# Own places for the parts of xu, one place for two scratch tiles, and another table of biases in a planned kernel

## The chip, the cores and the metric

The kernel runs on one core of a Trainium2 chip. The time is device microseconds (us) of one execution. TensorE is PE in the rows, VectorE is DVE, ScalarE is ACT, GpSimd is POOL, and SyncE, which issues the DMAs, is SP. A row's PEclk is the granted clock of TensorE as a share of full speed.

## The reference

Three computations follow one another, all in fp32, for 4 batches of 768 positions and 384 channels (8 heads of 48).

```python
# 1. attention with a complex decay; a is scaled so that |a| <= 0.999
for t in range(S):
    new_re = ar * S_re - ai * S_im
    new_im = ar * S_im + ai * S_re
    S_re, S_im = new_re + kv, new_im          # kv = outer(k_t, v_t)
    y[:, :, t] = einsum('bhd,bhde->bhe', q[:, :, t], S_re)
# 2. mixing over the positions (rank 32), then a channel MLP 384 -> 1536 -> 384
u = x + (x^T @ U @ V)^T
x = u + relu(u @ w_ch1) @ w_ch2
# 3. a gate from a causal convolution of 5 taps
gate = sigmoid(sum_k conv_w[k] * x shifted by 4 - k)
out = (gate * (x @ w_val)) @ w_out
```

## The kernel before, in words

**The work.** The attention goes through 12 units, three for each batch b, of 256 positions each, named by their first position: (b, 0), (b, 256), (b, 512). A unit (`attention`, line 763) reads the decay into z, normalises it (xa), forms running products over groups of 8 positions (the prefix steps, lines 809 to 814: two products s1 and s2, then z), carries the products over the groups (the phase steps, lines 820 to 892: un, tot, cx, fs, t), scales q and k with them (xc), transposes them on PE (pst, into qT and kT), and runs chunks of 128 positions as matmuls: pss (q times k), masked by DVE to mt; pkv, the state st; py, the output yt. yt goes to memory, and by pxt, xo and pxu into xu, the product of x and U.

The rest (`moe`, line 1042) goes by batch and by half hf of 384 positions; (0,1) is half 1 of batch 0. At the start of a batch, xu is split into a large part xh and a small part xl = xu - xh, and both are copied into xuh (lines 1043 to 1053). For each half: three matmuls pu of xuh; DVE adds them to the input xt; ACT makes the large part of m3u and DVE the small one (`pair`, line 1036). Matmuls of full precision are three passes: large by large, large by small, small by large. Twelve blocks then go through ph (9 matmuls), hp (large part on ACT, small on DVE) and px (9 matmuls). Behind the last px, DVE adds px to xt; ACT makes the large parts of m3x, DVE the small ones; ACT does the first tap and DVE the four others of each of the three convolutions (g, 12 steps in all), ACT the sigmoid; pv (27 matmuls), g times pv, m3g; po (27 matmuls), and the result ob is written.

**The weights** come as 64-bit numbers. DVE and ACT turn them into fp32 (`single`, line 678: wt by one TENSOR_SCALAR and two SCALAR_TENSOR_TENSOR for each of 28 tiles) and split them into two parts (w) while the first attention units run.

**Places.** `T` (line 521) asks for a tile in a named place with a number of buffers. A tile that takes a used buffer waits until all operations on the holder before have ended (lines 145 to 155). Before, xh takes a place of m3 (three buffers, shared with m3u, m3x and m3g), xl and jkx one of ob (two buffers, shared with the results). The phase steps' scratch has a place of its own, t1; the prefix steps use s1 and s2.

**The order.** No operation is issued when the program's text names it. `add` (line 176) records it; `order` (line 244) lays all operations out as a list schedule, and `emit` issues each engine's operations in that order. An operation's urgency is its longest remaining path, plus a bias from the table `URGE` (line 117), by kind and engine: "m00V" is DVE's work of half (0,0), "a10P" PE's work of the first unit of batch 1, "sV", "w0A" small inputs and weights.

```python
bias = [self.URGE.get(op.kind + op.eng, 0.0) for op in self.ops]
...
start, end = self.lay([x + y for x, y in zip(urgency, bias)])
...
return sorted(self.ops, key=lambda o: (o.start, o.i))
```

So a place that changes its name takes some waits away and adds others, and another table changes the order on all engines. On an engine, instructions run in the order in which they were issued.

Of the kernel before, what the change touches and what calls it, by code (L numbers as in the profile page):

```python
# [10 lines left out]
F32 = mybir.dt.float32  # L11
F32R = mybir.dt.float32r
# [88 lines left out]
class Program:  # L101
# [32 lines left out]
    }  # L134

    def hop(self, d, u):
# [363 lines left out]
def chunked_path(ctx, tc, outer, q, k, v, a_re, a_im, moe_U, moe_V, w1, w2, w_val, conv_w, w_out, out):  # L500
# [260 lines left out]
    XN = DM * RK // 128  # L761
# [461 lines left out]
```

## Time and profile before

| | |
|---|---|
| time, median of 3 | 757.41 us (753.73 to 758.91) |
| profiled execution | 754.51 us, span 752.6 us |
| PE busy | 627.3 us (83%), 4354 matmuls |
| DVE busy | 622.9 us (83%), 1545 instructions |
| ACT busy | 449.0 us (60%), 1110 instructions |
| mean granted clock of PE | 0.94 |
| chain that ended last | PE 53%, DVE 30%, DMA 6%, ACT 5% |

The profile shows one execution. Its rows of a timeline give start, duration, engine, line, operation, output and inputs, count, and in brackets the idle time of the engine before the row and what ended it. A row of windows gives the length, the busy time of each engine, the mean granted clock, the share of DMA and its rate. The first moe half, (0,0), gets its first m3u at 163.4 us, and the later halves at 239.8, 334.4, 405.2, 491.1, 550.9 and 643.1 us; PE's last px ends at 723.1 us. Stages are cut at these marks.

### The profile page before, as it was taken

Reading aid. Unit: us, or ns where it says so; the run is one execution under the profiler, and the core shown is the slowest. Engines: PE = TensorE matmul, PEld = TensorE weight load, DVE = VectorE, ACT = ScalarE, POOL = GpSimd, SP = SyncE. Lnnn points to the kernel's source line nnn. Section 1 sums busy time; section 2 is a strip of 40 time slices with the busy share of each in tenths; the row PEclk is TensorE's granted clock in tenths of the full one; section 3 lists DMA queues with packets and bytes.
Section 4 is the critical chain, followed back from the end, with each engine's and each line's share of the span. In section 5 each row is a group of like instructions: output and inputs, shape, how many; then the busy total and the mean of one; then the engine's idle time right before and its main releaser. Section 6 shows DMA issues by size and latency. Waiting matters only on the chain.

```text
span 752.6 us, 12213 instructions
## 1 busy us (share of the span) xinstructions
PE 627.3 (83%) x4354; PEld 577.5 (77%) x4354; DVE 622.9 (83%) x1545; ACT 449.0 (60%) x1110; POOL 2.7 (0%) x31
## 2 busy tenths in 40 slices
PE   0002959969978999889989999899899999999994
PEld 0002848749967989869988999789799998899984
DVE  5999999999999989799799899995799885515261
ACT  6899877673585564774665565851865355414243
POOL 1000000000000000000000000000000000000000
PEclk9999559869997999889999999999999999999997
DMA  5992315520521361430411544303124331100001
GB/s 120 305 369 65 76 21 138 126 54 0 139 51 53 85 151 35 126 101 22 127 43 54 148 112 130 84 23 105 43 74 120 82 84 33 54 0 1 1 32 36
DMA packets 74676, 64.39 MB, mean 86 GB/s; under 512 B 46704, under 2 KB 62064, under 8 KB 74608
## 3 DMA queue, kind: packets, MB, share of 16 engines
q1 hardware_dynamic: 74608, 63.54, 31.4%
q8 instruction: 36, 0.59, 0.3%
q14 instruction: 32, 0.26, 0.1%
HBM read 47.00 MB, written 16.52 MB: 84 GB/s over the span
## 4 chain that ended last, share of the span: by engine, by line
PE 53%; DVE 30%; DMA 6%; ACT 5%; SPq 3%; issue 2%; DVEq 0%; ACTq 0%
PE ph L600 18%; PE px L600 16%; DVE g L567 4%; PE po L600 3%; DVE z L551 3%; DVE xc L551 3%; PE pst L621 3%; PE py L612 3%; SPq L631 3%; PE pss L600 3%; DVE s L551 3%; DVE wt L567 2%; DVE xa L551 2%; PE pv L600 2%; PE pkv L612 2%
## 5 line engine op out<-in xcount | busy, mean ns | idle before, releaser
L600 PE MATMUL ph<-m3u,w 128*128 128x384 f32 x864 | 210.6, 353 | 4.2 <-ACT m3u L589 2.5
L600 PE MATMUL px<-hp,w 128*128 128x384 f32 x864 | 201.1, 343 | 0.6 <-DVE xt L551 0.4
L600 PEld LDWEIGHTS ph<-m3u,w 128*128 128x128 f32 x864 | 157.1, 194 | 10.9 <-ACT m3u L589 4.4
L600 PEld LDWEIGHTS px<-hp,w 128*128 128x128 f32 x864 | 153.1, 188 | 3.5 <-issue 1.7
L589 ACT ACTIVATE hp<-ph 128x384 fp32r<-128x384 f32 x96 | 46.7, 489 | 110.2 <-PE ph L600 100.4
L567 DVE SCALAR_TENSOR_TENSOR hp<-ph,hp 128x384 fp32r<-128x384 f32 x96 | 52.8, 552 | 58.8 <-ACT hp L589 58.3
L600 PE MATMUL pss<-qT,kT 96*128 96x128 f32 x384 | 54.7, 290 | 1.9 <-ACT qT L589 1.9
L551 DVE TENSOR_TENSOR s<-xa,z 128x192 f32<-128x192 f32 x168 | 54.3, 348 | 0.8 <-ACT z L589 0.3
L600 PEld LDWEIGHTS pss<-qT,kT 96*128 96x128 f32 x384 | 51.1, 202 | 4.0 <-ACT qT L589 2.6
L567 DVE SCALAR_TENSOR_TENSOR g<-xt,cw,g 128x384 f32<-128x384 f32 x96 | 52.9, 609 | 0.4 <-ACT g L589 0.3
L600 PE MATMUL pv<-m3x,w 128*128 128x384 f32 x216 | 45.6, 352 | 6.3 <-DVE m3x L551 5.1
L621 PE MATMUL pst<-eye_r,xc 128*96 128x128 f32 x192 | 32.1, 295 | 20.1 <-DVE rt L551 17.8
L589 ACT ACTIVATE xa<-xa,cb 128x384 f32<-128x384 f32 x72 | 42.9, 610 | 4.9 <-DVE xa L567 3.2
L600 PEld LDWEIGHTS pv<-m3x,w 128*128 128x128 f32 x216 | 37.1, 190 | 9.6 <-DVE m3x L551 7.0
L621 PEld LDWEIGHTS pst<-eye_r,xc 128*96 128x96 f32 x192 | 24.0, 137 | 23.0 <-ACT xa L589 18.0
L589 ACT ACTIVATE kT<-pst 96x512 f32<-96x512 f32 x48 | 27.3, 593 | 21.2 <-PE pst L621 21.0
L612 PE MATMUL py<-mt,vt 128*64 128x128 f32 x384 | 39.5, 296 | 0.1
L612 PEld LDWEIGHTS pkv<-vt,ks 128*96 128x96 f32 x320 | 34.0, 186 | 5.8 <-DVE mt L551 3.6
L612 PE MATMUL pkv<-vt,ks 128*96 128x48 f32 x320 | 34.5, 267 | 4.0 <-DVE mt L551 3.1
L551 DVE TENSOR_TENSOR mt<-pss,cmask 128x512 f32<-128x512 f32 x48 | 32.5, 683 | 5.6 <-PE pss L600 5.2
L612 PE MATMUL py<-qT,st 96*64 96x128 f32 x320 | 35.3, 301 | 0.6 <-ACT xo L589 0.6
L621 PE MATMUL psT<-eye_r,qd 128*96 128x128 f32 x24 | 5.3, 297 | 36.0 <-ACT qd L589 36.0
(161 smaller groups left out, 1178.8 us busy)
## 6 DMA issues: line engine op xcount, KB each, us to landing
raw<-in_moe_w_ch_dram SPq DMA_DIRECT2D x24, 384.0 KB, 7.2
kd<-z SPq DMA_DIRECT2D x18, 384.0 KB, 3.9
ks<-kd SPq DMA_DIRECT2D x15, 384.0 KB, 4.2
z<-in_a_re_dram SPq DMA_DIRECT2D x12, 384.0 KB, 4.5
z<-in_a_im_dram SPq DMA_DIRECT2D x12, 384.0 KB, 5.3
qk<-in_k_dram SPq DMA_DIRECT2D x12, 384.0 KB, 4.2
qk<-in_q_dram SPq DMA_DIRECT2D x12, 384.0 KB, 5.1
vt<-in_v_dram SPq DMA_DIRECT2D x24, 192.0 KB, 2.9
```

Source lines behind the costliest of these rows:

```text
L551: e, cost, lambda: engines[e].tensor_tensor(out=real(o), in0=real(a), in1=real(b), op=op), views(a, b), [o]
L567: lambda: nc.vector.scalar_tensor_tensor(out=real(o), in0=real(a), scalar=real(s), in1=real(b), op0=o0, op1=o1),
L589: return nc.scalar.activation(real(o), real(a), func, scale=real(scale), **kw)
L600: "P", cost, lambda: nc.tensor.matmul(real(o), real(lhsT), real(rhs), start=start, stop=stop),
L612: r = nc.tensor.matmul(ro[idx], real(lhsT), real(rhs), start=start, stop=stop)
L621: op = g.add("P", cost, lambda: nc.tensor.transpose(real(o), real(a), real(idn)), views(a, idn), [o])
L631: "S", cost, lambda: nc.sync.dma_start(real(o), real(a)), views(a), views(o), lat=1700.0 + time - cost
```

## The change

Three things are edited. In `moe`, xh gets the place "xh" and xl and jkx the place "xl", each with one buffer. In `attention`, five scratch tiles go from the place t1 to s2. And nearly all numbers of the table URGE are others (16 lines before and 17 after, of which two on each side are shown).

```diff
@@ -115,22 +115,23 @@
 
 
     URGE = {
-        "a00P": 514500.0, "a00S": 3500.0, "a00V": 2000.0, "a01A": 193500.0, "a01P": 3000.0, "a01S": -46500.0,
-        "a02P": 80000.0, "a02S": 2500.0, "a02V": 1500.0, "a10P": 78500.0, "a10S": -6000.0, "a10V": -5000.0,
...
+        "a00P": -54500.0, "a00V": 2000.0, "a01A": -1500.0, "a01P": -163000.0, "a01S": -35000.0, "a02P": 9000.0,
+        "a02S": 23500.0, "a02V": 1000.0, "a10A": -26500.0, "a10P": 14500.0, "a10S": -15000.0, "a10V": -5000.0,
...
@@ -818,7 +819,7 @@
         if NB == 2:
             mid = z[:, RB - 1]
             rt = T("p1", [128, 2, D], F32, "s1", "rt" + n)
-            sp = T("p1", [128, 2, 2, D], F32, "t1", "t1" + n)
+            sp = T("p1", [128, 2, 2, D], F32, "s2", "t1" + n)
             mul("V", sp, end.unsqueeze(1).to_broadcast([128, 2, 2, D]), mid.unsqueeze(2).to_broadcast([128, 2, 2, D]))
             sub("V", rt[:, 0], sp[:, 0, 0], sp[:, 1, 1])
             add("V", rt[:, 1], sp[:, 0, 1], sp[:, 1, 0])
@@ -838,7 +839,7 @@
         gs = [P2, 2, 2, 4 * H]
         uv = un.rearrange("p w c (i g) -> p w c i g", i=4)
         for i in range(1, 4):
-            sp = T("p1", gs, F32, "t1", "s1" + n)
+            sp = T("p1", gs, F32, "s2", "s1" + n)
             mul("V", sp, uv[:, :, :, i], uv[:, 0, :, i - 1].unsqueeze(2).to_broadcast(gs))
             add("V", uv[:, 0, :, i], sp[:, 0], sp[:, 1])
         act(uv[:, 1, 0, 1:4], uv[:, 0, 1, 1:4], scale=-1.0)
@@ -850,13 +851,13 @@
         act(c0[:, :, 0:H], prev)
         hs = [P2, 2, 2, H]
         for gg in range(4):
-            sp = T("p1", hs, F32, "t1", "s1" + n)
+            sp = T("p1", hs, F32, "s2", "s1" + n)
             mul("V", sp, uv[:, :, :, 3, gg * H : (gg + 1) * H], prev.unsqueeze(2).to_broadcast(hs))
             prev = c0[:, :, (gg + 1) * H : (gg + 2) * H]
             add("V", prev, sp[:, 0], sp[:, 1])
         js = [P2, 2, 3, 4 * H]
         for c in range(2):
-            sp = T("p1", js, F32, "t1", "s1" + n)
+            sp = T("p1", js, F32, "s2", "s1" + n)
             mul("V", sp, uv[:, :, c, 0:3], c0[:, :, 0 : 4 * H].unsqueeze(2).to_broadcast(js))
             s0, s1 = (sp[:, i].rearrange("p i (g h) -> p i g h", h=H) for i in range(2))
             add("V", cx[:, c, :, 1:4].rearrange("p g i h -> p i g h"), s0, s1)
@@ -885,7 +886,7 @@
         act(fs_[:, 0, 1:3], psC)
         act(fs_[:, 0, 0], psC[:, 1], scale=-1.0)
         if NB == 2:
-            sp = T("p1", [128, 2, 2, D], F32, "t1", "t1" + n)
+            sp = T("p1", [128, 2, 2, D], F32, "s2", "t1" + n)
             ps_ = [128, 2, D]
             mul("V", sp[:, 0], fs_[:, 0, 1:3], mid[:, 0:1].to_broadcast(ps_))
             mul("V", sp[:, 1], fs_[:, 0, 0:2], mid[:, 1:2].to_broadcast(ps_))
@@ -1042,16 +1043,16 @@
     def moe(b):
         xu = xus[b]
         xuh = T("p1", [128, DM], F32R, "xuh", f"xuh_{b}")
-        xh = T("p3", [128, XN], F32R, "m3", f"xh_{b}")
+        xh = T("p1", [128, XN], F32R, "xh", f"xh_{b}")
         act(xh, xu)
-        xl = T("p2", [128, XN], F32, "ob", f"xl_{b}")
+        xl = T("p1", [128, XN], F32, "xl", f"xl_{b}")
         sub("V", xl, xu, f32(xh))
         for i in range(DM // XN):
             s, o = slice(RK * i, RK * (i + 1)), slice(XN * i, XN * (i + 1))
             for j in range(2):
                 act(xuh[RK * j : RK * (j + 1), o], xu[s])
                 tsc(xuh[RK * (j + 2) : RK * (j + 3), o], xl[s], 1.0, None, ALU.mult)
-        jk = T("p2", [128, XN], F32, "ob", f"jkx_{b}")
+        jk = T("p1", [128, XN], F32, "xl", f"jkx_{b}")
         act(jk, xu, AF.Identity, bias=cb[:, 7:8], scale=0.0, accum=xflag[:, b : b + 1])
         xts[b] = []
         for hf in range(NH):
```

No operation is added or taken away. Where the order differs is shown at three places.

DVE, the prefix steps of unit (0,0) at the start of the program. Before, with conversions of weights (wt, w) between them:

```order
L579 TENSOR_SCALAR wt2_250<-raw2_223 128x384
L551 TENSOR_TENSOR z_0_0_92<-s1_0_0_243,s2_0_0_248 128x2x96
L567 SCALAR_TENSOR_TENSOR wt2_250<-raw2_223,wt2_250 128x384
L551 TENSOR_TENSOR s1_0_0_259<-xa_0_0_148,z_0_0_92 128x192
L551 TENSOR_TENSOR s2_0_0_262<-xa_0_0_148,z_0_0_92 128x192
L551 TENSOR_TENSOR w0_245<-wt0_191,w0_245 128x384
L551 TENSOR_TENSOR z_0_0_92<-s1_0_0_259,s2_0_0_262 128x2x96
L579 TENSOR_SCALAR wt1_271<-raw1_231 128x384
L551 TENSOR_TENSOR s1_0_0_275<-xa_0_0_148,z_0_0_92 128x192
L551 TENSOR_TENSOR s2_0_0_277<-xa_0_0_148,z_0_0_92 128x192
L567 SCALAR_TENSOR_TENSOR wt1_271<-raw1_231,wt1_271 128x384
L551 TENSOR_TENSOR z_0_0_92<-s1_0_0_275,s2_0_0_277 128x2x96
```

And now:

```order
L552 TENSOR_TENSOR s1_0_0_239<-xa_0_0_148,z_0_0_92 128x192
L552 TENSOR_TENSOR s2_0_0_241<-xa_0_0_148,z_0_0_92 128x192
L552 TENSOR_TENSOR z_0_0_92<-s1_0_0_239,s2_0_0_241 128x2x96
L552 TENSOR_TENSOR s1_0_0_246<-xa_0_0_148,z_0_0_92 128x192
L552 TENSOR_TENSOR s2_0_0_248<-xa_0_0_148,z_0_0_92 128x192
L552 TENSOR_TENSOR z_0_0_92<-s1_0_0_246,s2_0_0_248 128x2x96
L552 TENSOR_TENSOR s1_0_0_252<-xa_0_0_148,z_0_0_92 128x192
L552 TENSOR_TENSOR s2_0_0_254<-xa_0_0_148,z_0_0_92 128x192
L552 TENSOR_TENSOR z_0_0_92<-s1_0_0_252,s2_0_0_254 128x2x96
L552 TENSOR_TENSOR s1_0_0_257<-xa_0_0_148,z_0_0_92 128x192
L552 TENSOR_TENSOR s2_0_0_261<-xa_0_0_148,z_0_0_92 128x192
L552 TENSOR_TENSOR z_0_0_92<-s1_0_0_257,s2_0_0_261 128x2x96
```

The conversions no longer stand between the steps; each z is read by the s1 directly behind it, and reads the s2 directly ahead.

PE, the boundary from batch 0 to batch 1 (po of half (0,1), pu and ph of half (1,0)). Before:

```order
L612 MATMUL pxu_1_512_3487<-xo_1_512_0_3403,u2_151 32x96 x4
L600 MATMUL po_0_1_3384<-wo2_2239,m3g_0_1_3398 128x384 x2
L612 MATMUL pxu_1_512_3487<-xo_1_512_1_3483,u2_151 32x96 x4
L600 MATMUL po_0_1_3504<-w27_2209,m3g_0_1_3354 128x384 x3
L600 MATMUL po_0_1_3504<-wo2_2239,m3g_0_1_3382 128x384 x3
L600 MATMUL po_0_1_3504<-wo2_2239,m3g_0_1_3398 128x384 x3
L600 MATMUL pu_1_0_3558<-vst_195,xuh_1_3522 128x384
L600 MATMUL pu_1_0_3563<-vst_195,xuh_1_3522 128x384
L600 MATMUL pu_1_0_3568<-vst_195,xuh_1_3522 128x384
L600 MATMUL ph_1_0_3576<-m3u_1_0_3571,w0_245 128x384
L600 MATMUL ph_1_0_3581<-m3u_1_0_3571,w0_245 128x384
```

And now:

```order
L601 MATMUL po_0_1_3470<-wo2_2199,m3g_0_1_3481 128x384 x2
L601 MATMUL po_0_1_3467<-wo2_2199,m3g_0_1_3481 128x384
L601 MATMUL po_0_1_3470<-wo2_2199,m3g_0_1_3481 128x384
L601 MATMUL po_0_1_3490<-w27_2166,m3g_0_1_3437 128x384 x2
L601 MATMUL po_0_1_3490<-wo2_2199,m3g_0_1_3457 128x384 x3
L601 MATMUL pu_1_0_3542<-vst_190,xuh_1_3494 128x384
L601 MATMUL po_0_1_3490<-wo2_2199,m3g_0_1_3481 128x384
L601 MATMUL pu_1_0_3547<-vst_190,xuh_1_3494 128x384
L601 MATMUL po_0_1_3490<-wo2_2199,m3g_0_1_3481 128x384 x2
L601 MATMUL ph_1_0_3561<-m3u_1_0_3554,w0_336 128x384
L601 MATMUL ph_1_0_3563<-m3u_1_0_3554,w0_336 128x384
```

Two pu now stand between the last po, and the third (not shown) comes behind five ph. The last pxu of unit (1,512), which stood ahead of the last nine po, now stands ahead of all 27.

DVE, the gate of half (0,1): the taps g and the small parts m3x. Before (the two other m3x follow the taps, three rows further down):

```order
L567 SCALAR_TENSOR_TENSOR g_0_1_3224<-xt_0_1_1628,cw_235,g_0_1_3224 128x384
L551 TENSOR_TENSOR z_2_0_2771<-s1_2_0_3203,s2_2_0_3206 128x2x96
L567 SCALAR_TENSOR_TENSOR g_0_1_3224<-xt_0_1_1628,cw_235,g_0_1_3224 128x384
L551 TENSOR_TENSOR m3x_0_1_3240<-xt_0_1_1628,m3x_0_1_3240 128x384
L567 SCALAR_TENSOR_TENSOR g_0_1_3248<-xt_0_1_1628,cw_235,g_0_1_3248 128x384
L567 SCALAR_TENSOR_TENSOR g_0_1_3224<-xt_0_1_1628,cw_235,g_0_1_3224 128x384
L567 SCALAR_TENSOR_TENSOR g_0_1_3248<-xt_0_1_1628,cw_235,g_0_1_3248 128x384
L567 SCALAR_TENSOR_TENSOR g_0_1_3267<-xt_0_1_1628,cw_235,g_0_1_3267 128x384
L567 SCALAR_TENSOR_TENSOR g_0_1_3248<-xt_0_1_1628,cw_235,g_0_1_3248 128x384
L567 SCALAR_TENSOR_TENSOR g_0_1_3267<-xt_0_1_1628,cw_235,g_0_1_3267 128x384
L567 SCALAR_TENSOR_TENSOR g_0_1_3224<-xt_0_1_1628,cw_235,g_0_1_3224 128x384
```

And now:

```order
L568 SCALAR_TENSOR_TENSOR g_0_1_3230<-xt_0_1_1650,cw_231,g_0_1_3230 128x384
L568 SCALAR_TENSOR_TENSOR g_0_1_3235<-xt_0_1_1650,cw_231,g_0_1_3235 128x384
L568 SCALAR_TENSOR_TENSOR g_0_1_3218<-xt_0_1_1650,cw_231,g_0_1_3218 128x384
L568 SCALAR_TENSOR_TENSOR g_0_1_3230<-xt_0_1_1650,cw_231,g_0_1_3230 128x384
L568 SCALAR_TENSOR_TENSOR g_0_1_3235<-xt_0_1_1650,cw_231,g_0_1_3235 128x384
L552 TENSOR_TENSOR m3x_0_1_3241<-xt_0_1_1650,m3x_0_1_3241 128x384
L552 TENSOR_TENSOR m3x_0_1_3246<-xt_0_1_1650,m3x_0_1_3246 128x384
L552 TENSOR_TENSOR m3x_0_1_3253<-xt_0_1_1650,m3x_0_1_3253 128x384
L552 TENSOR_TENSOR mt_1_512_0_3281<-pss_1_512_0_3233,cmask_110 128x512
L552 TENSOR_TENSOR mt_1_512_0_3285<-pss_1_512_0_3237,cmask_110 128x512
```

The small part that stood behind the second tap now stands behind the twelfth, with the two others.

## Rows read from the trace of the kernel before

**Rows 1.** Windows by stage: span, busy time of each engine, TensorE clock, DMA.

```profile
20.00:163.40 143.40, 74.32 (x578) 62.35 (x579) 142.61 (x391) 117.92 (x341) 0.00 (x0) 0.82 0.51 149
163.40:239.80 76.40, 70.50 (x443) 65.74 (x444) 75.55 (x194) 43.45 (x103) 0.11 (x1) 0.91 0.23 55
239.80:334.40 94.60, 87.18 (x638) 78.66 (x637) 84.42 (x213) 59.79 (x140) 0.00 (x0) 0.96 0.39 103
...
491.10:550.90 59.80, 57.32 (x334) 55.13 (x334) 46.73 (x114) 31.45 (x71) 0.11 (x1) 0.97 0.20 54
```

**Rows 2.** Timeline of DVE: start, duration, engine, line, operation, tiles, count, idle before.

```profile
30.81 0.34 DVE L579 TENSOR_SCALAR wt<-raw 128x384 int32<-128x384 int32 x1
31.08 0.61 DVE L551 TENSOR_TENSOR s<-xa,z 128x192 f32<-128x192 f32 x2
31.62 0.34 DVE L579 TENSOR_SCALAR wt<-raw 128x384 int32<-128x384 int32 x1
...
41.62 0.16 DVE L551 TENSOR_TENSOR tot<-s 96x16 f32<-96x16 f32 x1
41.70 0.54 DVE L567 SCALAR_TENSOR_TENSOR wt<-raw,wt 128x384 int32<-128x384 int32 x1
42.17 0.17 DVE L551 TENSOR_TENSOR s<-un,tot 96x32 f32<-96x32 f32 x1
42.38 0.17 DVE L551 TENSOR_TENSOR tot<-s 96x16 f32<-96x16 f32 x1
42.58 0.19 DVE L551 TENSOR_TENSOR s<-un,tot 96x32 f32<-96x32 f32 x1
```

**Rows 3.** Timeline of PE, gate of half (0,1) and boundary to batch 1.

```profile
309.66 2.67 PE L600 MATMUL pv<-m3x,w 128*128 128x384 f32 x10 [2.14 <-DVE m3x L551]
...
331.65 0.42 PE L600 MATMUL pu<-vst,xuh 128*128 128x384 f32 x1 [1.42 <-DVE xuh L579]
332.32 0.41 PE L600 MATMUL pu<-vst,xuh 128*128 128x384 f32 x1 [0.25 <-DVE xuh L579]
333.25 0.45 PE L600 MATMUL pu<-vst,xuh 128*128 128x384 f32 x1 [0.52 <-ACT xuh L589]
334.19 0.65 PE L600 MATMUL ph<-m3u,w 128*128 128x384 f32 x2 [0.49 <-ACT m3u L589]
```

**Rows 4.** Timeline of PE, boundary from batch 1 to 2.

```profile
488.15 0.86 PE L600 MATMUL pu<-vst,xuh 128*128 128x384 f32 x2 [0.33 <-DVE xuh L579]
489.89 0.44 PE L600 MATMUL pu<-vst,xuh 128*128 128x384 f32 x1 [0.88 <-ACT ob L589]
491.13 3.20 PE L600 MATMUL ph<-m3u,w 128*128 128x384 f32 x9 [0.80 <-ACT m3u L589]
```

**Rows 5.** Windows behind the gate, the two boundaries, and in the tail.

```profile
310.00:318.00 8.00, 8.00 (x58) 7.69 (x56) 5.09 (x14) 4.04 (x8) 0.00 (x0) 0.57 0.21 48
334.00:342.00 8.00, 7.61 (x24) 6.21 (x25) 6.25 (x21) 3.53 (x14) 0.00 (x0) 0.57 0.01 3
490.00:496.00 6.00, 5.20 (x19) 4.65 (x20) 5.09 (x13) 3.37 (x12) 0.00 (x0) 0.72 0.15 52
730.00:734.00 4.00, 2.47 (x13) 1.89 (x12) 3.38 (x7) 3.95 (x8) 0.00 (x0) 1.00 0.27 98
```

**Rows 6.** Chain of waits, early: start, duration, what.

```profile
21.28 9.54 DMA z<-in_a_re_dram
```

**Rows 7.** The page's DMA issues.

```profile
raw<-in_moe_w_ch_dram SPq DMA_DIRECT2D x24, 384.0 KB, 7.2
```

**Rows 8.** Timeline of DVE, gate of half (0,1).

```profile
303.76 5.37 DVE L567 SCALAR_TENSOR_TENSOR g<-xt,cw,g 128x384 f32<-128x384 f32 x10
309.06 1.02 DVE L551 TENSOR_TENSOR m3x<-xt,m3x 128x384 fp32r<-128x384 f32 x2
```

**Rows 9.** Timeline of PE, tail.

```profile
731.34 0.44 PE L600 MATMUL pv<-m3x,w 128*128 128x384 f32 x1 [0.82 <-ACT ob L589]
732.50 4.65 PE L600 MATMUL pv<-m3x,w 128*128 128x384 f32 x25 [0.71 <-DVE m3x L551]
```

29 rows, old and new, of the table URGE are left out of this document.

## The prediction

> **What bounds the kernel now.** I read the page first (VectorE, "DVE", and TensorE, "PE", are both busy for 83% of the span), and then the same span cut into stages, because an average over stages with different limits says little. The cuts are the moments at which a moe half gets its first input m3u. In [rows 1] the reader is to see two regimes. From 20.0 to 163.4 us DVE is busy 142.61 of 143.40 us, and from 163.4 to 239.8 it is busy 75.55 of 76.40: there DVE's queue is the clock of the kernel, and a step added to it or taken from it counts in full, as long as PE can follow. Later PE leads: 87.18 of 94.60 us in the stage from 239.8 on, 57.32 of 59.80 from 491.1 on, with DVE idle for 10.2 and 13.1 us of these stages. There, DVE work is hidden, and what costs time is PE waiting or running at its lower clock.
>
> Third, I read the timeline of DVE for the step from one start to the next [rows 2]: a 128x384 operation steps 0.47 us (41.70 to 42.17), a conversion by TENSOR_SCALAR 0.27 (30.81 to 31.08), a 128x192 operation 0.27 (two in 0.54). The last rows show one more price. A tiny operation with a stranger behind it steps 0.08 us (41.62 to 41.70); the same kind with its own reader directly behind it steps 0.20 to 0.21. So a dependent neighbour costs some 0.115 us more.
>
> Fourth, the timeline of PE at the batch boundaries [rows 3, 4] and the granted clock beside it [rows 5].
>
> **What the change does.** The new places and the moved scratch add and remove no operation; all counts stay the same. What moves is the order, on every engine, because the whole table of biases is another one. So I count by stage, from the two orders.
>
> **1. The DVE-bound start.** Up to the first m3u of half (0,0), the new order holds 8 conversions wt and 3 operations w more than the old. Eight wt, as five at 0.47 and three at 0.27, make 3.2 us, three w at 0.47 make 1.4. Ten more dependent neighbours, at 0.115, make 1.15; the prefix chain of unit (0,0) is one place, whose steps stood with conversions between them and now stand bare. Two small phase operations leave (-0.4). Sum +5.3 us: the first m3u comes at 168.7. The next stage, up to the m3u of half (0,1), loses the same 11 (-4.6), four xa of 384 (-1.9), two xa of 768 (taken as twice 384, -1.9) and two s (-0.5), and gains three small ones (+0.8): -8.1. Together DVE reaches the second mark 2.7 us sooner. PE has to follow: it was busy 70.50 us of that stage, partly at half clock (mean 0.91), so that at full clock it needs some 64 us (70.50 x 0.91), against the 68.3 us that would be left (76.4 - 8.1). It can, but with little air, so I leave 1.0 of the 2.7 to PE and take -1.7. Bounds: -2.7, and +5.3 if the stage stays as long as it was.
>
> Behind the moved conversions stand their transfers. On SP's queue nine weights stood ahead of six attention transfers, the first of which took 9.54 us to land [rows 6]; now these six stand ahead of the first weight. A weight takes 7.2 us to land [rows 7], and DVE asks for the first one later than before (wt0 stands 27 places further down its queue). I put this at 0, with 2 us as the upper bound.
>
> Here a page has something to say. The Trainium skill ("VectorE: DVE Perf Modes", section "The DRAIN you can't avoid") tells that eight chained copies took 13.88 us with a semaphore after each and the same without, "the semaphore costs nothing extra here". By it the ten neighbours would be free and the first mark would lie at 167.6. The trace speaks against it for steps this short [rows 2], so the sum goes by the rows.
>
> **2. Boundary from batch 0 to 1.** Before, PE ran the last nine po of half (0,1) in one piece, and then waited for the small inputs of the next batch: 1.42 + 0.25 + 0.52 + 0.49 = 2.7 us over pu and the first ph [rows 3]. After this the clock stood at a mean of 0.57 for 8 us, mostly its lower level of 1.2 GHz, with 7.61 busy [rows 5]: (1 - 0.57) x 7.61 = 3.3 us lost. Together 6.0. In the new order the last contribution to xu (pxu) stands ahead of all 27 po, and two of the three pu between the last po. The 24 po between pxu and the first pu cover DVE's and ACT's work on xu. What isn't covered is the path from pu through the sum and m3u to ph, which took 2.5 us (331.65 to 334.19) and has only three po and a pu in it now. So I take half, -3.0; bounds 0 and -6.0.
>
> **3. Boundary from 1 to 2.** The same pattern: 0.33 + 0.88 + 0.80 = 2.0 us of waits [rows 4] and (1 - 0.72) x 5.20 = 1.5 us of clock [rows 5]. In the new order pu stands between the po here too. Half of 3.5 is -1.8; bounds 0 and -3.5. The boundary from 2 to 3 is written as it was: 0.
>
> **4. Stage (2,0).** 11.3 us of DVE work of attention unit 3_256 move into it from the stages on either side. DVE was idle for 13.1 us there [rows 1], so it fits, but barely, and the idle pieces lie between answers to ph that PE waits for. I take +1.5; bounds 0 and +6 (half of the work on the path). What leaves the next stage gives nothing, since PE is its bound.
>
> **5. Gates and tail.** In the gate of half (0,1) the first low part of m3x was made after 2 of the 12 taps; now all three come behind the twelfth, as in (1,1). Ten taps last 5.37 us [rows 8]. PE waited 2.14 us for the two late ones before [rows 3] and will wait longer, but for one piece. Since the last low part itself comes no later, I count 0 (bounds -0.5 and +3.4, one more spell such as that from 310 to 318 [rows 5]). In the tail, pv of (3,0) leave the place behind the last px, where they filled PE's time while DVE did the taps. DVE saves the same 1.9 us there. Today's two waits, 0.82 and 0.71 [rows 9], become one of about 2.5 us; the clock held at 1.00 through the short ones [rows 5]. A spell of half clock costs up to 3.3; I take a quarter, +0.8; bounds 0 and +3.3.
>
> **6. The scratch** in s2 instead of t1 is written and read by DVE alone, whose queue is in order. Both ends are 0, apart from the neighbours counted above.
>
> **Sum:** -1.7 - 3.0 - 1.8 + 1.5 + 0.8 = -4.2 us, against the profiled execution (754.51, span 752.6): 750.3. That execution lies 1.6 us below the mean of the four times shown (756.1) and 2.9 below their median of three, so a new median should lie near **752**.
>
> **Rivals.**
> - **Much faster (0.27), 746.** The boundaries give all (-6.0 and -3.5), and the DVE gain comes through (-2.7) while 4 and 5 keep +2.3: -9.9, or 746.2. For it: waits of 0.82 and 0.71 us left the clock alone [rows 5, 9], so fewer waits may keep it up altogether. Against it: the 2.5 us path from pu to ph is not shortened.
> - **Nothing moves (0.22), 757.** Waits change places only: the boundaries' gain is eaten by longer waits in the gates, where the low parts stand behind the taps. For it: after the start PE is the bound and its work is the same.
> - **Slower (0.16), 759.** PE starts (0,0) 5.3 us later and does not regain it, because in that stage its matmuls are spread thinner over the attention's products and each spell waits on DVE as before. Place: the stage from the first m3u on. Price: +5.3 in place of -1.7, so +2.8 in sum. It decides from the point at which that stage stays longer than 73.6 us (239.8 + 2.5 - 168.7), where the other terms' -2.5 is used up; with the weights' transfers late as well (+2) and stage 4 at its bound, it passes 765.
> - **Chained steps are free (0.05), 751.** On this kernel, DVE's in-order queue would then give 1.15 us more at the start, and nothing later where PE leads. The page named above gives that rule; its effect would lie within what a measurement can tell.
>
> My forecast itself has 0.30. **Range:** 742 (the faster rival without the losses of 4 and 5, 743.9, and some 2 us of the spread between runs) to 761 (the slower rival and its late transfers). One per cent, 7.6 us, is about what a measurement can tell from no change. Faster than 749.8: the faster rival and the low edge of my own, 0.29. Slower than 765: the upper part of the slower rival, 0.11. Between them 0.60.
>
> **What would show it.** In the profile of the changed kernel: the first m3u near 168.7 and the second near 237 to 238; dependent neighbours in the prefix chain stepping about 0.385 instead of 0.27; no wait for xuh ahead of pu at either boundary, one of 1 to 2 us ahead of ph, and a clock above 0.9 behind it; DVE nearly without idle time in stage (2,0); one wait of 2 to 3 us in the tail. I am wrong if the stage of half (0,0) stays at 76 us, if the spells at half clock are as many in other places, or if PE waits for the hp of ph in stage (2,0).

## The result and the profile after

The changed kernel takes **746.75 us** (median of 4, 746.11 to 747.59), the kernel before, beside it, 755.57; the ratio is 0.9889, interval 0.9851 to 0.9927. The forecast was 752, in a range of 742 to 761: the direction was right, and the size came out at 1.1%, where 752 against the median before of 757.41 meant 0.7%. The time is that of the rival "much faster" (746). A second set gave 747.83 us (746.77 to 749.06), ratio 0.9887 (0.9824 to 0.9951).

Profile against profile the span falls from 752.6 to 744.7 us. A mark is the moment at which DVE starts the first m3u of a half, and a stage runs from one mark to the next. The windows of the stages in the changed kernel, cut at the marks as in [rows 1] (span, busy time and count of PE, weight loads, DVE, ACT, POOL, then the clock and the DMA):

```profile
169.70:238.20 68.50, 67.43 (x444) 62.49 (x445) 67.52 (x178) 39.31 (x93) 0.11 (x1) 0.97 0.24 61
238.20:332.70 94.50, 87.05 (x635) 78.86 (x633) 87.33 (x212) 61.07 (x147) 0.00 (x0) 0.95 0.39 100
332.70:398.30 65.60, 63.52 (x410) 59.40 (x410) 61.40 (x155) 38.77 (x90) 0.11 (x1) 1.00 0.23 63
...
483.60:544.30 60.70, 58.30 (x349) 54.65 (x351) 57.12 (x134) 34.86 (x82) 0.11 (x1) 1.00 0.20 57
```

Against the marks of before this makes the following table (stage lengths in us; the first stage runs from 0):

| stage up to the first m3u of | before | after | difference | forecast |
|---|---|---|---|---|
| (0,0) | 163.4 | 169.7 | +6.3 | +5.3 |
| (0,1) | 76.4 | 68.5 | -7.9 | -7.0 |
| (1,0), with the gate of (0,1) and the boundary | 94.6 | 94.5 | -0.1 | } -3.0 |
| (1,1), with the clock behind the boundary | 70.8 | 65.6 | -5.2 | } |
| (2,0), with the boundary 1 to 2 | 85.9 | 85.3 | -0.6 | -1.8 |
| (2,1) | 59.8 | 60.7 | +0.9 | +1.5 |
| (3,0) | 92.2 | 90.5 | -1.7 | 0 |
| to the end | 109.5 | 109.9 | +0.4 | +0.8 |
| sum | 752.6 | 744.7 | -7.9 | -4.2 |

In the second row of the table the mean clock is 0.97 where it was 0.91, and PE's idle time is 1.1 us where it was 5.9: PE follows the shorter queue of DVE. In the last row of the windows, stage (2,0), DVE is busy for 57.12 us of 60.70 (before 46.73 of 59.80), and the stage is only 0.9 us longer.

The prefix chain of unit (0,0), on the timeline of DVE, has the bare steps that the order showed:

```profile
22.28 0.63 DVE L552 TENSOR_TENSOR s<-xa,z 128x192 f32<-128x192 f32 x2
22.94 0.36 DVE L552 TENSOR_TENSOR z<-s,s 128x192 f32<-128x192 f32 x1
23.33 0.63 DVE L552 TENSOR_TENSOR s<-xa,z 128x192 f32<-128x192 f32 x2
```

The product z comes 0.39 us behind the second s (each row of s holds two: 0.66 less 0.27), and the next s 0.39 us behind z. A 128x192 step with a stranger behind it took 0.27 [rows 2]. So some 0.12 us for a dependent neighbour holds for this size too. The page of the Trainium skill ("VectorE: DVE Perf Modes", section "The DRAIN you can't avoid"), by which it is free, does not hold for steps this short.

The two boundaries on PE's timeline, batch 0 to 1, and 1 to 2:

```profile
331.06 0.44 PE L601 MATMUL pu<-vst,xuh 128*128 128x384 f32 x1
...
331.51 0.37 PE L601 MATMUL pu<-vst,xuh 128*128 128x384 f32 x1
...
332.76 1.39 PE L601 MATMUL ph<-m3u,w 128*128 128x384 f32 x5 [0.53 <-ACT m3u L590]
```

```profile
480.75 0.34 PE L601 MATMUL pu<-vst,xuh 128*128 128x384 f32 x1
...
481.82 0.44 PE L601 MATMUL pu<-vst,xuh 128*128 128x384 f32 x1 [0.21 <-ACT ob L590]
...
483.62 0.62 PE L601 MATMUL ph<-m3u,w 128*128 128x384 f32 x2 [0.82 <-ACT m3u L590]
```

Of the four waits of [rows 3] (2.7 us) one of 0.53 us is left, of the three of [rows 4] (2.0 us) two of together 1.03. The windows behind the gate, the two boundaries, and in the tail show more, in the column of the clock:

```profile
310.00:318.00 8.00, 7.58 (x53) 6.65 (x53) 6.63 (x20) 3.11 (x7) 0.00 (x0) 0.54 0.13 25
332.00:340.00 8.00, 7.19 (x34) 5.30 (x33) 6.93 (x25) 4.32 (x16) 0.00 (x0) 1.00 0.20 70
483.00:489.00 6.00, 4.87 (x23) 3.76 (x23) 5.89 (x17) 4.49 (x18) 0.00 (x0) 1.00 0.14 47
722.00:726.00 4.00, 1.88 (x10) 1.55 (x10) 3.52 (x7) 3.95 (x7) 0.00 (x0) 1.00 0.27 98
```

Behind both boundaries the clock stays at 1.00 where it was 0.57 and 0.72 [rows 5]. Behind the gate of (0,1) it does not: 0.54. The waits there and in the tail:

```profile
307.64 1.97 PE L601 MATMUL pv<-m3x,w 128*128 128x384 f32 x5 [3.87 <-DVE m3x L552]
```

```profile
722.88 0.45 PE L601 MATMUL pv<-m3x,w 128*128 128x384 f32 x1 [0.82 <-ACT ob L590]
724.63 4.62 PE L601 MATMUL pv<-m3x,w 128*128 128x384 f32 x25 [1.31 <-DVE m3x L552]
```

The gate's wait grew from 2.14 to 3.87 us, and the tail's two from 1.53 in all to 2.13, with the clock at 1.00.

The marks of a kernel are those of its one profiled execution. For the changed kernel its time (746.89) is close to the median; in three of the experiments below it lies 3 to 6 us above the median: 761.41 against 756.97 with the old places, 763.55 against 757.74 with the start alone, 756.85 against 753.54 with the order up to (1,1).

### The profile page after: what moved, and what is told of

It reads as the page before. It is cut to its first block, busy times and chain, and to the rows that moved or that the text cites. A ratio compares the mean times of both kernels' runs of the same rounds, so it can differ in the third digit from the quotient of the medians.

```text
span 744.7 us, 12217 instructions
## 1 busy us (share of the span) xinstructions
PE 624.0 (84%) x4354; PEld 574.7 (77%) x4354; DVE 626.5 (84%) x1545; ACT 447.2 (60%) x1110; POOL 2.7 (0%) x31
## 4 chain that ended last, share of the span: by engine, by line
PE 55%; DVE 26%; ACT 9%; DMA 5%; SPq 2%; issue 2%; ACTq 0%
PE ph L601 18%; PE px L601 17%; DVE g L568 4%; PE pv L601 4%; PE pst L622 3%; PE po L601 3%; DVE z L552 3%; PE py L613 3%; DVE xc L552 3%; DVE s L552 3%; SPq L632 2%; PE pss L601 2%; ACT ab L590 2%; DVE xa L552 2%; PE pkv L613 2%
## 5 line engine op out<-in xcount | busy, mean ns | idle before, releaser
L601 PE MATMUL px<-hp,w 128*128 128x384 f32 x864 | 205.1, 343 | 0.5 <-ACT hp L590 0.5
L601 PEld LDWEIGHTS ph<-m3u,w 128*128 128x128 f32 x864 | 155.3, 192 | 12.5 <-ACT m3u L590 5.1
L601 PE MATMUL pv<-m3x,w 128*128 128x384 f32 x216 | 50.3, 357 | 8.9 <-DVE m3x L552 7.9
L601 PEld LDWEIGHTS pv<-m3x,w 128*128 128x128 f32 x216 | 38.0, 194 | 12.4 <-DVE m3x L552 10.3
L622 PE MATMUL pst<-eye_r,z 128*96 128x128 f32 x192 | 31.8, 310 | 3.1 <-DVE z L552 1.8
```

Source lines behind the costliest of these rows:

```text
L601: "P", cost, lambda: nc.tensor.matmul(real(o), real(lhsT), real(rhs), start=start, stop=stop),
L622: op = g.add("P", cost, lambda: nc.tensor.transpose(real(o), real(a), real(idn)), views(a, idn), [o])
```

## The experiments

In most of them the program's operations are those of the changed kernel, and only the order is another one: `order` returns a list that is written into the kernel, and each engine runs its operations in that order.

```diff
-        return sorted(self.ops, key=lambda o: (o.start, o.i))
+        return [self.ops[i] for i in ids]
```

Theory: the change gains by moving DVE work out of the stage where DVE is the clock, and by boundaries that only the new places allow. Rivals: the places do nothing and the table does all; or the start alone does it; or work is only put off. The reverse of the first, the new places with the old table, was not run.

**The old places, with the new order.**

```diff
-        xh = T("p1", [128, XN], F32R, "xh", f"xh_{b}")
+        xh = T("p3", [128, XN], F32R, "m3", f"xh_{b}")
-        xl = T("p1", [128, XN], F32, "xl", f"xl_{b}")
+        xl = T("p2", [128, XN], F32, "ob", f"xl_{b}")
-        jk = T("p1", [128, XN], F32, "xl", f"jkx_{b}")
+        jk = T("p2", [128, XN], F32, "ob", f"jkx_{b}")
```

> The changed kernel's order on every engine, but xh again in a place of m3 and xl, jkx in places of ob (the scratch stays in s2). Only what these places forbid is moved: on PE 5 operations, on DVE 25, on ACT 32, all at the three batch boundaries. Theory 'the places make the boundaries': xl of batch 1 has to wait for the second result ob of half (0,1) (ends at 331.39 us in the changed kernel) and its transfer (1.9 to 2.3 us), so it comes at about 333.4 instead of 328.77; the same at the next boundary (483.8 instead of 479.07). PE then waits some 4.6 us at each for pu, and falls to its lower clock behind it: two times 4.6, plus 1.5 to 3.3 each, 12 to 16 us slower than the changed kernel where nothing covers it, 6 at least: 753 to 763 us. Theory 'the table alone': the rest of the order carries the gain, and this run stays within 2 us of the changed kernel (745 to 749).

Measured: 756.97 us, ratio 1.0018 (0.9993 to 1.0044): the whole gain is gone. On DVE's timeline, on PE's, and in a window of it:

```profile
334.71 0.26 DVE L672 TENSOR_TENSOR xl<-xu,xh 128x96 f32<-128x96 f32 x1 [3.29 <-DMA out_dram<-ob]
```

```profile
336.00 1.11 PE L721 MATMUL pu<-vst,xuh 128*128 128x384 f32 x2 [2.81 <-DVE xuh L700]
```

```profile
338.00:342.00 4.00, 3.98 (x12) 3.89 (x13) 3.21 (x12) 1.83 (x6) 0.00 (x0) 0.50 0.14 51
```

xl waits 3.29 us for the transfer of a result, PE 2.81 us for pu, and then PE runs at 0.50, its lower level. In this profile the first ph of (1,0) is 5.3 us later than in the changed kernel, that of (1,1) 7.9, that of (2,0) 9.4; all marks up to the last px of (0,1) agree within 0.4. By the code, xh and xl (128x96 fp32) take 384 bytes of a partition each, and t1, which the scratch gave up, had 768: the new places have exactly its room. That they would not have fitted beside it is not shown.

In the trace of before xl waits for no transfer at any batch start: there DVE's only idle time ahead of an xl is one of 0.6 us, for xh. So it is the new order that needs the new places; what these alone would bring under the old table is not shown.

**One old place at a time.** The same edit for xl and jkx alone, and for xh alone.

> The changed kernel's order with xh in its own place, but xl and jkx again in places of ob; what that forbids is moved (5 operations on PE, 25 on DVE, 14 on ACT). With both old places, xl of batch 1 started at 334.71 us behind 3.29 us of waiting for the transfer of a result. Theory 'it is xl': the same here, first ph of (1,0) at 337 to 338.5 against 333, lower clock behind it, and 753 to 758 us in all. Theory 'it is xh': within 2 us of the changed kernel (747.8 beside the last set).

> The changed kernel's order with xl and jkx in their own place, but xh again in a place of m3, which the po of the first m3g of the half before must have left (4 operations on DVE and 18 on ACT moved). Theory 'it is xl': xh waits for po, not for a transfer: it comes 2 to 4 us later than 328.0, pu and first ph of (1,0) 1 to 3 us later, and the run is 1 to 4 us slower than the changed kernel (748 to 752). Theory 'it is xh': as slow as with both old places (755 to 758).

Measured: xl in ob 757.98 us, ratio 1.0031 (1.0001 to 1.006); xh in m3 754.80, ratio 1.0001 (0.9976 to 1.0026). The rows of xl on DVE in the first, of xh on ACT and of pu and ph on PE in the second:

```profile
335.97 0.26 DVE L672 TENSOR_TENSOR xl<-xu,xh 128x96 f32<-128x96 f32 x1 [3.57 <-DMA out_dram<-ob]
```

```profile
331.16 0.28 ACT L710 ACTIVATE xh<-xu 128x96 fp32r<-128x96 f32 x1
```

```profile
332.76 0.41 PE L721 MATMUL pu<-vst,xuh 128*128 128x384 f32 x1 [1.26 <-DVE xuh L700]
...
335.24 1.92 PE L721 MATMUL ph<-m3u,w 128*128 128x384 f32 x5 [1.26 <-ACT m3u L710]
```

The transfer makes xl the worse of the two, as forecast. But xh alone costs 7 us, not 1 to 4: its first ph of (1,0) is 2.5 us late, as expected, the lower clock behind it makes that 3.3 by the last px, and the gate of (1,0) 4.8 by the first ph of (1,1). Up to the last px of (2,0) it grows to 9.1, with the boundary 1 to 2, which was not expected at all.

**Where in the program the gain lies.** Two orders put together from both kernels: the changed one's up to a mark, then that of before for what is left.

> The changed kernel's order up to the first m3u of half (0,1), then the order of the kernel before for all that is left, in the places of the kernel before. Theory 'stage by stage': the first m3u of (0,0) at 169.7 us and that of (0,1) at 238.2, as in the changed kernel, and all later marks as before, shifted by 1.6 to 1.9 us: 1.7 us faster than before (ratio 0.998). Rival 'the start is the cause of all': the better clock and order of the start carries over, and the run comes within 2 us of the changed kernel (ratio 0.989). Rival 'the start is paid for later': the moved work comes due in the next stage and the run is not faster than before.

> The changed kernel's order up to the first m3u of half (1,1), with its places, then the order of the kernel before (4 DVE operations moved where the shared scratch demands it). Theory 'stage by stage': marks as in the changed kernel up to (1,1), first ph of (1,1) 6.1 us sooner than before, and 6 us faster in all (ratio 0.992); the rest, 1.4 us at the boundary from 1 to 2 and some 0.4 later, is missing. Rival: the gain up to there is given back in the stages that follow (ratio over 0.996), because work was only pushed on.

Measured: 757.74 us, ratio 1.0014 (0.9985 to 1.0043), and 753.54, ratio 0.9971 (0.9950 to 0.9992). Both missed what I expected, and the first shows why, on PE's timeline:

```profile
247.79 1.01 PE L721 MATMUL ph<-m3u,w 128*128 128x384 f32 x2 [5.30 <-ACT m3u L710]
```

What the changed order leaves for later, the order of before holds first. So eight DVE steps of unit (1,512) came ahead of the m3u of (0,1), 5.65 us of DVE's queue (242.12 to 247.77), and PE stood still for 5.30. That I had not thought of when I cut there. (In this profile the first ph of (0,1) is 9.4 us later than in the changed kernel; the other 4 come from a late ks, told in the last section.) The same happens at the cut of the second: DVE adds the first pu of (1,1) to xt at 399.30 and makes m3u only at 406.03, with attention steps between. These runs do not tell the stages apart; they point to what the put-off steps are worth, which the next two test.

**The put-off work by itself.** First the changed kernel with these eight steps moved back ahead of m3u; then the kernel before, in its own places, with only these steps put off.

In DVE's order the two edits read (a row for an operation, first the changed kernel's, then a piece of that of before):

```diff
 z_256
+xa_512
+xa_512
+xa_512
+xa_512
+xa_512
+xa_512
+s_1_512
+s_1_512
 m3u_1
-xa_512
 xt_1
...
 m3u_1
-xa_512
 xc_256
```

```diff
 s_1_256
-xa_512
 cx_256
-xa_512
-s_1_256
-xa_512
+s_1_256
...
 m3u_1
+xa_512
 z_256
```

> The changed kernel, but eight DVE steps of unit (1,512) (four xa of 384, two of 768, s1, s2) and four ACT steps between them stand ahead of the m3u of half (0,1) again, as in the kernel before; nothing else is moved. In the run of the start alone these eight took 5.65 us of DVE's queue and PE stood idle for 5.30 us. Theory 'work moved off the path': first ph of (0,1) 5 to 6 us later (243.5 to 244.5), of which the stage behind it gives back 1 to 3, since it has 5.7 us less DVE work now: 750 to 753 us in all. Rival 'only deferred': the whole is given back by the first ph of (1,0), and the run is within 1.5 us of the changed kernel.

> The kernel before, in its own places and with its own order, but for one thing taken over from the change: the eight DVE steps of unit (1,512) (and the z that reads the last two) stand behind the m3u of half (0,1) instead of inside the gate of half (0,0); the ACT steps between them move along (28 places on ACT, 57 on DVE, none on PE). In the changed kernel the reverse edit cost 6.9 us. Theory 'DVE's queue alone': m3u of (0,1) comes 5 to 6 us sooner than 239.8 and the run is 4 to 6 us faster than before (ratio 0.992 to 0.995). Theory 'PE was the bound at this mark': PE's last po of half (0,0) ended at 240.41 us, behind three waits (1.25, 2.89 and 0.94 us) and a spell of half clock in the gate, so an earlier m3u finds PE busy; only the waits for mt shrink by 0.5 to 1 us, first ph of (0,1) comes 1 to 2.5 us sooner, and the run is within 2.5 us of before (ratio over 0.9965). It needs the changed kernel's order of the gate on PE as well.

Measured: 754.15 us, ratio 0.9964 (0.9940 to 0.9988), and 759.15, ratio 1.0048 (1.0023 to 1.0073). The first ph that had to wait, in the one and in the other:

```profile
244.93 1.65 PE L721 MATMUL ph<-m3u,w 128*128 128x384 f32 x4 [5.74 <-DVE m3u L672]
```

```profile
240.42 0.62 PE L721 MATMUL ph<-m3u,w 128*128 128x384 f32 x2 [1.38 <-ACT m3u L710]
...
250.56 1.14 PE L721 MATMUL ph<-m3u,w 128*128 128x384 f32 x5 [1.58 <-DVE hp L688]
```

Moved back, the eight steps make PE wait for 5.74 us, and nothing of it is given back: the last px of (0,1) is 5.5 us later than in the changed kernel, the end 7.5. So the loop of (0,1) is PE's, and takes about the same time with 5.7 us more or less of DVE work beside it. Put off alone, the mark does come 2.7 us sooner, but PE then waits for m3u and, since the steps now stand ahead of hp, for hp, and the last px of (0,1) comes 2.9 us later than before. The run is slower by 0.5%; neither theory had that, though the second's bound (a ratio over 0.9965) holds. Work put off gains where it lies between PE's waits, and costs where it stands ahead of hp.

The 2 us that the run with the steps moved back loses beyond the 5.5 come for the most part from the gate of (1,0). PE has the same operations and the same three waits there in both kernels (0.18 or 0.19, 0.58, and 0.97 or 0.96 us). The pv behind the third, and the clock over them, first in the changed kernel, then with the steps moved back:

```profile
386.67 4.45 PE L601 MATMUL pv<-m3x,w 128*128 128x384 f32 x24 [0.97 <-DVE m3x L552]
```

```profile
386.00:392.00 6.00, 5.33 (x37) 5.32 (x38) 6.00 (x13) 4.12 (x9) 0.11 (x1) 1.00 0.02 6
```

```profile
392.42 6.01 PE L721 MATMUL pv<-m3x,w 128*128 128x384 f32 x24 [0.96 <-DVE m3x L672]
```

```profile
392.00:398.00 6.00, 5.58 (x23) 5.58 (x24) 5.19 (x11) 3.54 (x8) 0.11 (x1) 0.72 0.02 4
```

So the same waits left the clock at 1.00 in one kernel and not in the other, at a price of 1.6 us. In the gate of (1,0) the clock also held in the second set's run of the changed kernel and in those of the gate, of ks and of POOL below, and it fell in those of the old places, of xl, of xh and of the order up to (1,1) (0.61 to 0.65 over 3 us of these pv). What decides is open. The runs with an old place lose 7 to 11 us and this one 6 to 7, so that one of each together exceeds the whole gain of 8.8: they show that both parts are needed, not which share each has.

**The gate of (0,1).** The DVE order between the taps and behind m3x, and PE's to match:

```diff
 g_0_1
+mt_1_512_0
 g_0_1
 g_0_1
+mt_1_512_0
...
 m3x_0_1
 m3x_0_1
 m3x_0_1
-mt_1_512_0
-mt_1_512_0
+st1
```

> The changed kernel, with the gate of half (0,1) written in another order: mt of the next chunk between the taps, and py and pkv of that chunk on PE ahead of the pv that wait for the small parts of m3x; what follows of this unit (pss, mt, py, pxt, g times pv, m3g) is drawn ahead accordingly; 26 operations on PE, 55 on DVE, 24 on ACT stand elsewhere. Theory 'the gate is the last large loss': PE's wait of 3.87 us falls to 1 to 2, the spell of half clock from 309 to 317 (3.7 us lost) goes, and the run is 2 to 5 us faster than the changed kernel (742 to 745); it cannot be all of 6 since DVE has only some 3 us of idle time between 309 and 332. Rival: DVE is the bound there, and PE only waits elsewhere: within 1 us of the changed kernel.

Measured: 752.03 us, ratio 0.9959 (0.9927 to 0.9991), so 4 to 5 us slower than the changed kernel. Three rows of PE and one of DVE:

```profile
309.26 1.84 PE L721 MATMUL pv<-m3x,w 128*128 128x384 f32 x9 [1.27 <-DVE m3x L672]
...
320.51 0.37 PE L733 MATMUL pxu<-xo,u 128*32 128x96 f32 x8
...
333.19 0.69 PE L721 MATMUL pu<-vst,xuh 128*128 128x384 f32 x1 [4.12 <-DVE un L672]
```

```profile
328.13 0.24 DVE L672 TENSOR_TENSOR xu<-xu,pxu 128x96 f32<-128x96 f32 x1
```

The gate itself does what was meant: the wait falls to 1.27 us, the clock is 1.00 from 309 to 317 (0.50 in the changed kernel), and the last pxu comes at 320.51 instead of 326.41. But DVE adds it to xu only at 328.13 (327.67 in the changed kernel), behind the steps xa of the next unit, and PE idles for 4.12 us ahead of pu, with the clock at 0.70 from 333 to 341. Neither forecast came out, since the rival had it within 1 us. Its mechanism fits in part: in this order it is DVE's queue that sets when xu is ready, though DVE is not full there (busy 19.29 of the 23 us from 309 to 332).

**The transfer ks, and POOL.** Beside a run of the changed kernel as it is, one with two transfers ahead of the loads in front of them on SP's queue, and one with the small parts of the weights on POOL.

```diff
 qk_1_256
+ks_1_0_0
 z_1_512
 z_1_512
-ks_1_0_0
```

```diff
-                sub("V", to[key][:, 1], x, f32(to[key][:, 0]))
+                sub("G", to[key][:, 1], x, f32(to[key][:, 0]))
```

> The changed kernel again, as it is, on the chip and beside the runs of this set: 744 to 749 us, ratio 0.985 to 0.993. Marks (first ph of each half) within 1 us of the profile of the changed kernel, unless the transfer ks of unit (1,0) lands late as it did in the run of the start alone: then all marks from 238 on lie 3 to 4 us later.

> The changed kernel with one edit on SP's queue: the transfer ks of units (1,0) and (1,256) is issued ahead of the two loads z that stood before it (6 places moved, no other engine touched). Theory 'late ks': in the run of the start alone ks landed 7.3 us after its issue instead of 5.9, PE waited 1.88 us for it instead of 0.22, fell to its lower clock and lost 4 us. Issued first, ks has no loads of 384 KB ahead of it and lands in 3.5 to 4.5 us, by 217: pkv of unit (1,0) then never waits, the upper runs go, and the median falls by 0.5 to 2 us against the changed kernel beside it. Rival: ks shares the engines with the loads whichever is first, and nothing changes; or z, now later, is late for xa.

> The changed kernel in its own order, with the 28 subtractions w (small parts of the weights, 128x384) on POOL instead of DVE. 21 of them stand ahead of the first m3u, 0.47 us each. Theory 'DVE's queue is the clock of the start': the first m3u comes up to 9.9 us sooner than 169.7, and since PE is busy 67.85 of 68.92 us in the stage behind it, the whole run follows: 737 to 742 us. Rival 'POOL takes it back': POOL needs much longer for one, holds the three places of wt, or slows DVE's operations beside it, so that the first m3u does not move or comes later (747 to 765).

Measured: 747.83 (ratio 0.9887), 746.90 (0.9881, interval 0.9818 to 0.9943) and 755.69 us (1.0003, 0.9974 to 1.0031). pkv of unit (1,0) as it is, and with ks first:

```profile
220.03 1.53 PE L613 MATMUL pkv<-vt,ks 128*96 128x48 f32 x16 [0.57 <-DMA ks<-kd]
```

```profile
219.37 1.48 PE L733 MATMUL pkv<-vt,ks 128*96 128x48 f32 x16
```

The wait of 0.57 us goes, and the median differs by less than the runs scatter: no difference that can be told. With w on POOL, the group of w, and two rows of DVE beside each other in time:

```profile
L672 POOL TENSOR_TENSOR w<-wt,w 128x384 fp32r<-128x384 f32 x28 | 51.2, 1845 | 167.2 <-ACT w L710 143.0 <-DVE wt L688 22.4 <-DVE mt L672 1.2
```

```profile
80.82 0.16 DVE L672 TENSOR_TENSOR tot<-s 96x16 f32<-96x16 f32 x1
...
82.07 0.99 DVE L672 TENSOR_TENSOR tot<-s 96x16 f32<-96x16 f32 x1
```

POOL takes 1.85 us on average for what took DVE 0.47, and slows DVE: the same 96x16 product lasts 0.16 us alone and 0.99 beside POOL. The first m3u came 6.8 us later although DVE had 21 operations fewer ahead of it; DVE was busy for 163.4 us up to there, against 159.5. That DVE's queue is the clock of the start is not refuted by it, but not shown either.

**An order searched further.**

DVE's order begins to differ with its third conversion; a piece of it:

```diff
 vt
+xa_0
 vt
 xa_0
 vt
+xa_0
+vt
+xa_0
 vst
```

> The changed kernel's places and operations in an order searched further from its own, op by op, on the planner's own durations (those of the code: fixed costs and hops). What the experiments point to is in it: the gate of half (0,1) and the two boundaries closed up without the wait for xu that the rearranged gate had brought. Theory 'the losses that are left are losses of order': 740 to 745 us, first ph of (1,0) at 329 to 331 and of (3,0) at 626 to 630, instead of 333 and 635. Rival 'an order this tight breaks on the chip': transfers that land later than planned (ks, raw) leave PE waiting and at its lower clock, and it is 747 us or slower.

Measured: 745.32 us (744.27 to 746.94), ratio 0.9851 (0.9815 to 0.9886). It is the lowest of all, but its runs overlap with those of the changed kernel, and so do the intervals; the marks did not come where I had expected them (first ph of (1,0) at 334.4, of (3,0) at 636.5). I don't call it faster than the change.

## Why the prediction was right, and where its sizes were off

- **The start (step 1) was right in its mechanism, and its -1.7 partly by luck.** +5.3 and -1.7 were forecast for the two marks; +6.3 and -1.6 were measured. The count of DVE work was right to 0.1: DVE's busy time up to the first mark rose by 5.4 (154.1 to 159.5) and fell by 8.0 in the next stage (75.55 to 67.52). But DVE was idle 0.9 longer up to the first mark, for which there was no term, and the 1.0 left to PE was not needed: two misses of 1 us cancel. In the profile after DVE never waited for a weight (in the second set once, 0.5 us), so the late transfers cost nothing, as taken. The edit back showed that the put-off steps are worth their full DVE time at this mark, and that the stage behind does not give it back.
- **The boundary from 0 to 1 (step 2) was mis-sized.** It was halved to -3.0; waits and clock together gave -4.1. The waits fell by 2.1 of 2.7: what I took to be uncovered, the path from pu to ph, cost a wait of 0.53 us. The clock gave 2.0, and not the 3.3 of the working, from which half was taken. This is read from PE's loop of (1,0), from its first ph to its last px, with 273 recorded matmuls in both kernels: 48.02 us busy against 46.03. Most of the rest of the -5.2 in the table's row of (1,1) is neither: in the gate of (1,0), with its po, PE has 30 recorded matmuls fewer (2.0 us of busy time) and waits 0.75 less, and in the loop of (1,1) it has 41 more, with 3.0 us. So work moved from that row into the next. The four stretches (loop and gate of (1,0), loop and gate of (1,1) with the boundary), before and after:

```profile
334.19:382.41 48.22, 48.02 (x273) 45.55 (x273) 41.71 (x109) 24.75 (x64) 0.00 (x0) 0.93 0.22 58
382.41:404.91 22.50, 20.01 (x171) 17.73 (x169) 22.50 (x50) 15.43 (x30) 0.11 (x1) 1.00 0.25 66
404.91:462.92 58.01, 58.01 (x434) 54.58 (x435) 53.41 (x133) 32.56 (x81) 0.00 (x0) 1.00 0.46 119
462.92:491.13 28.21, 24.35 (x210) 20.98 (x207) 26.06 (x72) 24.16 (x62) 0.00 (x0) 1.00 0.37 97
```

```profile
332.76:379.07 46.31, 46.03 (x273) 43.20 (x275) 42.15 (x114) 25.70 (x64) 0.00 (x0) 1.00 0.24 66
379.07:398.82 19.75, 18.01 (x141) 16.65 (x142) 19.75 (x43) 13.01 (x26) 0.11 (x1) 1.00 0.22 61
398.82:459.86 61.04, 61.03 (x475) 57.02 (x475) 56.40 (x140) 35.73 (x86) 0.00 (x0) 1.00 0.45 119
459.86:483.62 23.76, 21.87 (x196) 19.41 (x194) 22.79 (x65) 20.76 (x51) 0.00 (x0) 1.00 0.38 103
```

- **That the clock holds behind short waits** was before me in [rows 9] and [rows 5] (waits of 0.82 and 0.71, clock 1.00), and I used it for a rival only. It is no sure thing either, as the gate of (1,0) shows above.
- **The places are what allows it.** The text counted the new places as bringing no operation and no time, and looked at the order alone. The run with the old places shows that the order loses its gain without them: xl comes behind a result's transfer, xh behind po. The forecast did not depend on it, but the explanation does.
- **The boundary from 1 to 2 (step 3):** its own waits fell by 1.0 (2.0 to 1.03), and all of PE's idle time in the gate and the boundary by 2.0 (3.86 to 1.89). The stage as a whole is only 0.6 shorter, since it took in the 3.0 us of PE work named above. The clock rose from 0.72 to 1.00, but the loop behind it is no shorter, so the 1.5 us that the working gave it can't be told apart there.
- **Stage (2,0) (step 4)** cost +0.9 where +1.5 was taken: DVE's busy time rose by 10.4 us, of 11.3 counted, and fitted into its idle time.
- **The gate (step 5)** was taken as 0. PE's wait grew by 1.7 us, but at the same low clock behind it; the last px of (0,1) came 0.6 us sooner than before, the first ph of (1,0) 1.4 sooner. **The tail** cost +0.4, with two waits still and not one, and the clock at 1.00, where +0.8 was taken.
- The stage of (2,1), the table's row of (3,0), fell by 1.7 us with no step for it. No run tells why.

Of the rivals, "much faster" has the time, but none of its three conditions in full: it added up to -9.9, from a mean of 756.1, and the span fell by 7.9. "Nothing moves" needed the gates to take the gain back; the wait in that of (0,1) grew by 1.7 us. "Slower" needed a stage of over 73.6 us behind the first m3u; it took 68.5. "Chained steps are free" is answered by the steps of 0.39 us.

## What to carry to other kernels

A tile's place is an edge in the schedule: a small tile that shares a rotating place with results can wait for a transfer to memory (3.29 and 3.57 us here), and where that tile starts a batch, PE waits and can then run at its lower clock (0.50 for 4 us here). Count DVE work by stage, before and after a reordering: moved from a stage that DVE bounds into a loop that PE bounds it was worth its whole time here, as long as it did not stand ahead of what PE waits for there. Price a wait with its clock, by rows at both levels, and check the price on a stretch with the same matmuls in both kernels. A row in which a wait of that length left the clock alone is a number for the sum, but with a chance beside it: the same waits went both ways here. And before a stage's difference is put down to a wait, compare its count of matmuls: work may only have moved to the next stage.

## What was not expected of the hardware

POOL and DVE slow each other. In the run with w on POOL, the 66 TENSOR_TENSOR operations of DVE that overlapped in time with a subtraction on POOL, up to the first m3u, lasted 560 ns on average, and the same operations in the changed kernel 424; for 17 SCALAR_TENSOR_TENSOR it was 631 and 480. POOL's own operation took 1.03 us at 90.81, where DVE was idle for 0.89 of it, and up to 10.3 us beside DVE's work.

The same order can meet a transfer at two times. In the run of the start alone, ks of unit (1,0) landed 7.3 us after its issue, in the changed kernel 5.9. PE waited 1.88 us instead of 0.22, the clock was 0.53 from 221 to 226 (1.00 from 218 to 226 in the changed kernel), mostly the lower level, and the po of the stage came 4 us later:

```profile
221.16 2.69 PE L733 MATMUL pkv<-vt,ks 128*96 128x48 f32 x16 [1.88 <-DMA ks<-kd]
```
